# At most four loads open at once on GpSimd's queue, in a linear-attention and token-mixing kernel

## The chip, the cores and the metric

The kernel runs on one core of one Trainium2 chip. The core has a matrix engine (TensorE, PE in the profile), a vector engine (VectorE, DVE), an activation engine (ScalarE, ACT), a general engine (GpSimd, POOL) and a synchronisation engine that issues transfers (SyncE, SP). Each works through its own list of instructions in order; semaphores tie the lists together. Sixteen DMA engines move data between the chip's memory (HBM) and the on-chip buffer (SBUF). TensorE writes to a second on-chip memory of 8 banks (PSUM).

The metric is the time of one execution on the device in microseconds (us); lower is better.

## What is computed

The inputs are q, k and v of shape (4, 8, 768, 64): 4 batches, 8 heads, 768 positions, 64 channels, in float32. The first half is linear attention with a decay `lam` per head, the second mixes the tokens of the result with each other. Cut to what matters:

```python
# attention, in blocks of 64 positions; lam is one number per head
intra = einsum('bhic,bhjc->bhij', qb, kb) * Dmask      # Dmask = lam ** (i - j), lower triangle
intra = einsum('bhij,bhjd->bhid', intra, vb)
inter = einsum('bhid,bhde->bhie', qb * lam ** (pos + 1), kv_state)
out[:, :, block] = intra + inter
kv_state = lam ** 64 * kv_state + einsum('bhsd,bhse->bhde', kb * lam ** (63 - pos), vb)

# token mixing; x is the attention's output as (batch, position, 512)
wq, wk = x @ w_q, x @ w_k                               # 512 -> 64
mixed = einsum('bst,btd->bsd', wq @ wk.T / 8, x)
return relu(mixed) @ w_out
```

## The kernel before, in words

The work is cut into 16 units, n = 0 to 15. A unit is one batch and one pair of heads (4 batches of 4 pairs); both heads lie side by side in 128 partitions or 128 columns. Units 0 to 3 are batch 0, and so on. When the four units of a batch are done, that batch's token mixing can run. The program handles blocks of 128 positions, six to a unit (NCH = 6), and takes the decay into q and v: q at position t is multiplied by lam to the power t, v by lam to the power -t, so that scores need only a triangular mask.

For each unit n there are three loads, `load_q`, `load_k` and `load_v` (lines 111 to 121), each into a buffer of its own (the pool `stage` has 16 of each, so no load waits for a buffer). They are issued by GpSimd, read float32 and write bfloat16, 192 KB on the chip each: q.n into `fq`, k.n into `fk`, v.n into `fv`. GpSimd also loads the three weight matrices (`load_wq`, `load_wk`, `load_wo`).

What sets the order is the text ORDER (lines 29 to 67), written out by hand: its words are read from left to right, each calls one function, and each function appends its instructions to the lists of the engines it uses. In a word, the number behind the dot is the unit, the number behind @ the PSUM bank, the letter behind the colon the engine (a: ScalarE, v: VectorE, p: GpSimd). Since engines run in parallel, only the order of the words that use one engine counts for that engine. For GpSimd that is: the loads q.0, k.0, v.0, q.1, k.1, v.1 (lines 144 to 153, ahead of ORDER), then the first three lines of ORDER. These hold all other loads and, between them, the words `sv.n:p`.

The steps that follow a unit's loads:

- Aq.n and Ak.n (`turn_q`, line 251; `turn_k`, line 260): TensorE transposes q.n and k.n, twelve matrix instructions each. These are the first uses of those loads.
- eq.n and ek.n (lines 266 and 234): VectorE or ScalarE take the transposes out of PSUM; eq.n multiplies by q's decay.
- sv.n (`scale_v`, line 239): v.n times its decay, in place in `fv`, on VectorE or GpSimd. In ORDER, GpSimd does n = 4, 5, 7, 9, 10, 11, 12, 13 and 14; VectorE does the rest. sv.4 stands behind v.7 in the list of GpSimd, sv.5 behind v.8, sv.7 behind v.10, sv.9 behind v.12, sv.10 behind v.13, sv.11 behind v.14, and sv.12, sv.13 and sv.14 behind v.15.
- S0.n and S1.n (line 277): the scores; M0, M1, Mc and Mm (lines 291, 306, 310) mask them.
- P.n (`states`, line 319): TensorE multiplies k.n by the scaled v.n into the running states. It needs sv.n.
- G.n takes the states out; I.n (line 347) and V.n (line 359) form the unit's output in PSUM; ex.n takes it to `xnat`; F.n (line 382) transposes it for the mixing.
- Q, K, Y, m and O with their evictions are the token mixing of a batch; O (line 508) ends in stores of `out` from SyncE.
- Z.n (line 528): n matmuls on a blank tile, early in the kernel, whose results aren't used.
- hold.14: a transfer of 64 elements out of `fk` of unit 14, issued by SyncE. Stores come behind it in SyncE's list.

The transfers of GpSimd's queue tell of their landing through eight semaphores, used in turn.

Of the kernel before, what the change touches and what calls it, by code (L numbers as in the profile page):

```python
# [9 lines left out]
BF16 = mybir.dt.bfloat16  # L10
# [16 lines left out]


ORDER = """
q.2 k.2 v.2 q.3 k.3 v.3 wq.0 wk.0 q.4 k.4 v.4 wo.0 q.5 k.5 v.5 q.6 k.6 v.6 q.7 k.7 v.7 sv.4:p q.8  # L30
k.8 v.8 sv.5:p q.9 k.9 v.9 q.10 k.10 v.10 sv.7:p q.11 k.11 v.11 q.12 k.12 v.12 sv.9:p q.13 k.13
v.13 sv.10:p q.14 k.14 v.14 sv.11:p q.15 k.15 v.15 sv.12:p sv.13:p sv.14:p hold.14 Aq.0@0 dq.2
eq.0@0 dq.3 Z.5@7 Ak.0@0 dq.1 ek.0@0:v Z.3@7 S1.0@0 sv.0:v S0.0@2 Mc.0@2 M1.0@0 Z.3@7 P.0@4 Aq.1@5
G.0@4:a Mm.0:v Z.1@7 I.0@0 eq.1@5 Ak.1@4 V.0@0 ek.1@4:v ex.0@0:a S0.1@4 sv.1:v S1.1@2 Mc.1@4 Z.1@7
F.0@0 M1.1@2 P.1@1 ef.0@0:a Aq.2@4 Mm.1:v G.1@1:a eq.2@4 Z.1@7 Ak.2@0 I.1@2 ek.2@0:v V.1@2 S1.2@0
# [35 lines left out]
def kernel(  # L71
# [11 lines left out]
    nc = tc.nc  # L83
    mm = nc.tensor.matmul

    consts = ctx.enter_context(tc.tile_pool(name="consts", bufs=1))
# [18 lines left out]
    def rows(n, src):  # L105
        b, kk = divmod(n, NP)
        return src[b, 2 * kk : 2 * kk + 2].rearrange("h (c p) d -> p h c d", p=128)

    fq, fk, fv, vn = {}, {}, {}, {}
# [9 lines left out]
    def load_v(n):  # L119
        fv[n] = stage.tile([128, 2, NCH, D], BF16, tag="fv", name="fv")  # L120
        nc.gpsimd.dma_start(out=fv[n], in_=rows(n, v))  # L121

    wqk = consts.tile([128, 4, 3 * DHY], BF16, name="wqk")
    wo = consts.tile([128, 4, HD], BF16, name="wo")
# [14 lines left out]
    def load_wo(_):  # L139
# [8 lines left out]
        row, pattern=[[0, 1]], base=1, channel_multiplier=1, allow_small_or_imprecise_dtypes=True  # L148
    )
    load_v(0)  # L150
    load_q(1)
    load_k(1)
    load_v(1)
    lam_all = consts.tile([128, H], F32, name="lam_all")
    nc.sync.dma_start(out=lam_all, in_=lam.partition_broadcast(128))
# [7 lines left out]
    one = consts.tile([128, 1], F32, name="one")  # L163
# [4 lines left out]
        out=ET[:, 0:CH], data0=step, data1=step, initial=0.0, op0=ALU.add, op1=ALU.bypass  # L168
    )
    for at, n in ((CH, CH), (2 * CH, 2 * CH), (4 * CH, 2 * CH)):  # L170
        nc.vector.tensor_tensor(
            out=ET[:, at : at + n], in0=ET[:, 0:n],
# [5 lines left out]
        out=ident.rearrange("e (p r) -> e p r", r=2), in0=natural,  # L178
# [4 lines left out]
        out=mask1, in0=ET[:, 0:CH], in1=row.to_broadcast([128, CH]), op=ALU.is_ge  # L183
# [4 lines left out]
    for r in range(2):  # L188
        nc.vector.tensor_tensor(
            out=token[R[r], :], in0=token[R[r], :],  # L190
# [5 lines left out]
        out=order.rearrange("e (p r) -> e p r", r=2), in0=natural,  # L196
# [5 lines left out]
        out=E6, in0=ET[:, ::CH], in1=row.to_broadcast([128, NCH]), op=ALU.add  # L202
# [69 lines left out]
    def scores(a):  # L272
        def one(n, o):
            for cc in range(3):
                c = slice((3 * a + cc) * CH, (3 * a + cc + 1) * CH)
                for hl in range(2):
                    mm(  # L277
                        PS[:, o + hl, cc * CH : (cc + 1) * CH],
                        kT[n][R[hl], c],
                        qT[n][R[hl], c],  # L280
                        start=True,
                        stop=True,
                        skip_group_check=True,
                    )

        return one
# [239 lines left out]
    def zeros(count, o):  # L526
# [4 lines left out]
    make_dq(0)  # L531
    make_dv(0)
    pieces = dict(
        q=load_q, k=load_k, v=load_v, wq=load_wq, wk=load_wk, cw=copy_wq, wo=load_wo, hold=hold, dq=make_dq, dv=make_dv,
        sv=scale_v, Aq=turn_q, Ak=turn_k, eq=turned_q, ek=turned_k, S0=scores(0), S1=scores(1),
        M0=masked(0), M1=masked(1), Mc=drawn, Mm=masked_late, P=states, G=summed, I=inter, V=values, ex=attended, F=flip,
        ef=flipped, eg=flipped_half, Q=mix_q, eQ=mixed_q, K=mix_k, eK=mixed_k, Kh=mix_k_half, ek2=mixed_k_half, Y=mix_y, YA=mixed_y, YB=crossed_y(0), YC=crossed_y(1), Qp=mix_q_part, m=mix_m,
# [38 lines left out]
```

## Time and profile before

| | |
|---|---|
| three timed runs, median | 99.39 us (99.37 to 99.69) |
| the profiled execution | 100.16 us |
| its span, first to last instruction | 98.4 us |
| granted TensorE clock, mean over the span | 0.99 |
| GpSimd: 16 issues of q, mean of one, and median to landing | 0.88 us, 7.5 us |
| GpSimd: 16 issues of k, the same | 1.05 us, 8.0 us |
| GpSimd: 16 issues of v, the same | 1.04 us, 8.0 us |
| GpSimd: 9 scalings of v | 1.51 us each |
| VectorE: 7 scalings of v | 1.00 us each |

Times inside the execution count from the span's start. "To landing" is the time from the start of the instruction that issues a transfer until its semaphore says that all of it has arrived. The page divides the span into 40 equal slices and gives each engine's busy share of a slice as a digit, 9 for 90% or more. "The chain" is followed back from the last instruction: at each step to what released it, or to the instruction before it on its engine. A row of a timeline gives start, duration, engine, line, operation, output and input, how many instructions are merged in it and, in brackets, the idle time ahead of it and what ended that.

### The profile page before, as it was taken

What the parts mean: (1) busy time and instruction counts of PE and PEld (TensorE: products, weight loads), DVE (VectorE), ACT (ScalarE), POOL (GpSimd) and SP (SyncE); (2) the same over time, 40 slices, a digit from 0 to 9 for tenths busy, and PEclk for the clock granted to TensorE, in tenths of its full rate; (3) what the DMA queues carried; (4) which work ended last, traced back from release to release, by engine and by line L of the source; (5) the groups of instructions that cost most, each with busy time, mean ns of one, the idle gap of its engine ahead of it and who ended that gap; (6) DMA issues with size and microseconds to landing.
All of it is one profiled execution on the core that took longest, in us unless ns stands there. A gap on an engine that the chain in (4) does not pass through costs nothing.

```text
span 98.4 us, 3425 instructions
## 1 busy us (share of the span) xinstructions
PE 88.8 (90%) x1469; PEld 56.3 (57%) x1469; DVE 72.0 (73%) x140; ACT 61.5 (63%) x101; POOL 61.5 (62%) x65
## 2 busy tenths in 40 slices
PE   5999898699989999999898899999999999999930
PEld 1345674567565667667566587777696754534400
DVE  5738892993889998998798499699999845544200
ACT  5576486158539358378557396776589992493440
POOL 5999996899579999999999999970000000000000
PEclk9999999999999999999999999999999999999996
DMA  0999999999999999999999999999950202545782
GB/s 1 95 143 163 165 156 167 159 167 190 182 164 162 169 161 164 166 162 163 168 162 164 166 164 161 174 223 402 372 188 6 107 7 107 213 154 217 286 308 101
DMA packets 67438, 16.60 MB, mean 169 GB/s; under 512 B 63840, under 2 KB 64352, under 8 KB 67424
## 3 DMA queue, kind: packets, MB, share of 16 engines
q0 software_dynamic: 63792, 10.10, 139.0%
q1 hardware_dynamic: 3632, 6.30, 17.0%
q8 instruction: 11, 0.18, 0.7%
q14 instruction: 3, 0.02, 0.1%
HBM read 20.19 MB, written 6.29 MB: 269 GB/s over the span
## 4 chain that ended last, share of the span: by engine, by line
PE 69%; DMA 8%; POOL 8%; DVE 5%; ACT 3%; issue 3%; POOLq 0%; ACTq 0%
PE ps L508 22%; DMA fv<-in_v_dram 8%; PE ps L359 6%; PE ps L277 6%; PE ps L382 5%; PE ps L319 5%; PE ps L260 5%; PE ps L404 4%; PE ps L251 4%; PE ps L455 3%; POOL fk L117 3%; PE ps L347 3%; POOL fq L113 3%; PE ps L479 2%; POOL fv L121 2%
## 5 line engine op out<-in xcount | busy, mean ns | idle before, releaser
L291 DVE TENSOR_TENSOR pr<-ps,mask 128x768 bf16<-128x768 f32 x28 | 25.9, 950 | 0.8 <-PE ps L277 0.7
L508 PE MATMUL ps<-wo,rmT 128*128 128x512 bf16 x96 | 23.6, 380 | 0.0
L117 POOL DMA_DIRECT2D fk<-in_k_dram x16 | 16.8, 1048 | 1.4 <-DMA wo<-in_moe_w_out_dram 1.3
L121 POOL DMA_DIRECT2D fv<-in_v_dram x16 | 16.7, 1044 | 1.4 <-DMA fv<-in_v_dram 1.0
L234 ACT COPY osb<-ps 128x512 f32<-128x512 f32 x19 | 11.2, 588 | 10.0 <-PE ps L508 8.9
L113 POOL DMA_DIRECT2D fq<-in_q_dram x16 | 14.1, 883 | 1.1 <-POOLq L560 0.8
L234 ACT CAST xnat<-ps 128x768 bf16<-128x768 f32 x13 | 10.4, 799 | 6.6 <-PE ps L359 6.2
L239 POOL TENSOR_TENSOR fv<-fv,DvI 128x768 bf16<-128x768 bf16 x9 | 13.5, 1512 | 0.0
L508 PEld LDWEIGHTS <-rmT 128*128 128x128 bf16 x96 | 8.3, 98 | 8.6 <-issue 0.7
L490 ACT ACTIVATE rmT<-ps 128x768 bf16<-128x768 f32 (+1 forms) x16 | 10.6, 722 | 0.2
L528 PE MATMUL ps<-blank 128*128 128x512 bf16 x29 | 9.5, 445 | 1.2 <-DVE blank L158 1.2
L266 DVE TENSOR_TENSOR qT<-ps,dq 128x768 bf16<-128x768 bf16 x16 | 8.8, 553 | 2.1 <-PE ps L251 2.0
L277 PE MATMUL ps<-qT,kT 64*128 64x128 bf16 x192 | 9.0, 218 | 0.4 <-DVE kT L234 0.3
L234 ACT COPY kT<-ps 128x768 bf16<-128x768 bf16 x9 | 7.2, 799 | 2.9 <-PE ps L260 2.4
L319 PE MATMUL ps<-fv,fk 128*64 128x128 bf16 (+4 forms) x160 | 7.8, 229 | 1.4 <-DVE fv L239 1.4
L359 PE MATMUL ps<-fv,pr 128*128 128x64 bf16 x192 | 8.5, 194 | 0.5 <-issue 0.5
L251 PE MATMUL ps<-ident,fq 128*64 128x128 bf16 x192 | 8.3, 221 | 0.3 <-DVE E L201 0.3
L260 PE MATMUL ps<-ident,fk 128*64 128x128 bf16 x192 | 8.3, 221 | 0.3
L239 DVE TENSOR_TENSOR fv<-fv,DvI 128x768 bf16<-128x768 bf16 x7 | 7.0, 1004 | 1.9 <-DMA fv<-in_v_dram 1.7
L319 PEld LDWEIGHTS <-fk 128*64 128x64 bf16 x160 | 5.9, 110 | 4.1 <-DVE fv L239 2.3
L277 PEld LDWEIGHTS <-kT 64*128 64x128 bf16 x192 | 5.6, 94 | 4.1 <-DVE kT L234 1.5
L359 PEld LDWEIGHTS <-pr 128*128 128x128 bf16 x192 | 6.8, 98 | 1.9 <-issue 0.8
(68 smaller groups left out, 131.2 us busy)
## 6 DMA issues: line engine op xcount, KB each, us to landing
out_dram<-osb SPq DMA_DIRECT2D x24, 256.0 KB, 2.1
fq<-in_q_dram POOLq DMA_DIRECT2D x16, 192.0 KB, 7.5
fk<-in_k_dram POOLq DMA_DIRECT2D x16, 192.0 KB, 8.0
fv<-in_v_dram POOLq DMA_DIRECT2D x16, 192.0 KB, 8.0
wo<-in_moe_w_out_dram POOLq DMA_DIRECT2D x1, 512.0 KB, 8.7
wqk<-in_moe_w_q_dram POOLq DMA_DIRECT2D x1, 64.0 KB, 7.6
wqk<-in_moe_w_k_dram POOLq DMA_DIRECT2D x1, 64.0 KB, 7.3
lam_all<-in_lam_dram SPq DMA_DIRECT2D x1, 4.0 KB, 2.5
```

The costliest lines, as they stand in the source:

```text
L113: nc.gpsimd.dma_start(out=fq[n], in_=rows_q(n))
L117: nc.gpsimd.dma_start(out=fk[n], in_=rows(n, k))
L121: nc.gpsimd.dma_start(out=fv[n], in_=rows(n, v))
L234: return (nc.scalar.copy if eng == "a" else nc.vector.tensor_copy)(out=to, in_=of)
L239: (nc.gpsimd if eng == "p" else nc.vector).tensor_tensor(out=vn[n], in0=fv[n], in1=DvI[:, 2 * kk : 2 * kk + 2, :].unsqueeze(3).to_broadcas ...
L251: nc.tensor.transpose(to.rearrange("e (t r p) -> e r t p", t=2, r=2)[:, r], fq[n][:, hl, a, r * D : (r + 1) * D], ident,)
L260: nc.tensor.transpose(PSH[R[hl], o, c * CH : (c + 1) * CH], fk[n][:, hl, c, :], ident)
L277: mm(PS[:, o + hl, cc * CH : (cc + 1) * CH], kT[n][R[hl], c], qT[n][R[hl], c], start=True, stop=True, skip_group_check=True,)
L291: nc.vector.tensor_tensor(out=pr[n, a].rearrange("j l (c i) -> j l c i", c=3), in0=PS[:, o : o + 2, 0:HALF].rearrange("j l (c i) -> j l c ...
L319: mm(to[R[hl], c:end, :], fk[n][:, hl, c, :], vn[n][:, hl, c, :].unsqueeze(1).to_broadcast([128, end - c, D]), start=(c == 0), stop=(c == ...
L359: mm(PS[:, o + hl, c * D : (c + 1) * D], pr[n, c // 3][:, hl, (c % 3) * CH : (c % 3 + 1) * CH], vn[n][:, hl, c, :], start=False, stop=(c = ...
L508: mm(PS[:, o, :], rmT[b][:, kt].rearrange("f n i -> f (n i)")[:, t * CH : (t + 1) * CH], wo[:, kt, :], start=(kt == 0), stop=(kt == 3),)
```

## The change

GpSimd copies one element of a load's buffer into a scratch tile, `landed`, before it issues another load. Since the copy reads the buffer, it can't run before that load has landed; the issue stands behind it in GpSimd's list. The copy ahead of a load reads the load four back among q, k and v: v.n-2 ahead of q.n, q.n-1 ahead of k.n, k.n-1 ahead of v.n. The first copy stands ahead of q.3. The weights' loads are issued without a copy of their own. All other words keep their order; `sv.n:p` stays directly behind the load that it followed.

```diff
 ORDER = """
-q.2 k.2 v.2 q.3 k.3 v.3 wq.0 wk.0 q.4 k.4 v.4 wo.0 q.5 k.5 v.5 q.6 k.6 v.6 q.7 k.7 v.7 sv.4:p q.8
-k.8 v.8 sv.5:p q.9 k.9 v.9 q.10 k.10 v.10 sv.7:p q.11 k.11 v.11 q.12 k.12 v.12 sv.9:p q.13 k.13
-v.13 sv.10:p q.14 k.14 v.14 sv.11:p q.15 k.15 v.15 sv.12:p sv.13:p sv.14:p hold.14 Aq.0@0 dq.2
+q.2 k.2 v.2 av.1 q.3 aq.2 k.3 ak.2 v.3 wq.0 wk.0 av.2 q.4 aq.3 k.4 ak.3 v.4 wo.0 av.3 q.5 aq.4 k.5 ak.4 v.5 av.4 q.6 aq.5 k.6 ak.5 v.6 av.5 q.7 aq.6 k.7 ak.6 v.7 sv.4:p av.6 q.8
+aq.7 k.8 ak.7 v.8 sv.5:p av.7 q.9 aq.8 k.9 ak.8 v.9 av.8 q.10 aq.9 k.10 ak.9 v.10 sv.7:p av.9 q.11 aq.10 k.11 ak.10 v.11 av.10 q.12 aq.11 k.12 ak.11 v.12 sv.9:p av.11 q.13 aq.12 k.13
+ak.12 v.13 sv.10:p av.12 q.14 aq.13 k.14 ak.13 v.14 sv.11:p av.13 q.15 aq.14 k.15 ak.14 v.15 sv.12:p sv.13:p sv.14:p hold.14 Aq.0@0 dq.2
...
+    landed = consts.tile([1, 1], BF16, name="landed")
+
+    def after(tiles):
+        def one(n):
+            nc.gpsimd.tensor_copy(out=landed, in_=tiles[n][0:1, 0, 0, 0:1])
+
+        return one
...
-        q=load_q, k=load_k, v=load_v, wq=load_wq, wk=load_wk, cw=copy_wq, wo=load_wo, hold=hold, dq=make_dq, dv=make_dv,
+        q=load_q, k=load_k, v=load_v, aq=after(fq), ak=after(fk), av=after(fv), wq=load_wq, wk=load_wk, cw=copy_wq, wo=load_wo, hold=hold, dq=make_dq, dv=make_dv,
```

That is 39 copies. On the other engines the list of instructions stays what it was.

## The prediction

> **What bounds the kernel now.** I read the page from the top, then the chain of waits in order of time, then GpSimd's own timeline, then the time to landing of single loads.
>
> ```profile
> span 98.4 us, 3425 instructions
> PE 88.8 (90%) x1469; PEld 56.3 (57%) x1469; DVE 72.0 (73%) x140; ACT 61.5 (63%) x101; POOL 61.5 (62%) x65
> ...
> POOL 5999996899579999999999999970000000000000
> ...
> DMA  0999999999999999999999999999950202545782
> ...
> PE 69%; DMA 8%; POOL 8%; DVE 5%; ACT 3%; issue 3%; POOLq 0%; ACTq 0%
> ```
>
> TensorE holds 90% of the span and 69% of the chain. GpSimd and the DMA engines are full too, but only for the first 65 to 72 us. So there are two stages: an early one in which loads decide, and a later one in which TensorE decides. The chain in order of time shows where they meet:
>
> ```profile
> 9.09 8.00 DMA fv<-in_v_dram
> 17.09 0.02 issue
> 17.11 0.97 DVE fv L239
> ...
> 31.89 0.57 PE ps L319 x10
> ...
> 43.23 0.38 PE ps L319 x10
> ```
>
> Until 17.09 us the chain is loads; afterwards nearly every piece is TensorE's. From 31.9 us to the last matmul at 94.4 us the windows give TensorE 60.8 us busy of 62.5 (11.10 of 11.10, 22.38 of 24.0, 27.35 of 27.4). It has no spare time there, and it works in program order, so a matmul that waits there moves the end. L319 is the state product P.n; its moving operand is the scaled v.n. For n = 4, 5, 7 and 9 to 14 GpSimd scales v.n (L239), between its own load issues:
>
> ```profile
> 22.36 0.84 POOL L113 DMA_DIRECT2D fq<-in_q_dram  x1
> 23.17 1.04 POOL L117 DMA_DIRECT2D fk<-in_k_dram  x1
> ...
> 27.36 1.02 POOL L117 DMA_DIRECT2D fk<-in_k_dram  x1 [1.32 <-DMA wo<-in_moe_w_out_dram]
> 28.73 1.01 POOL L121 DMA_DIRECT2D fv<-in_v_dram  x1 [0.35 <-issue]
> 29.75 1.48 POOL L239 TENSOR_TENSOR fv<-fv,DvI 128x768 bf16<-128x768 bf16 x1
> 31.17 0.89 POOL L113 DMA_DIRECT2D fq<-in_q_dram  x1
> ...
> 41.23 1.54 POOL L239 TENSOR_TENSOR fv<-fv,DvI 128x768 bf16<-128x768 bf16 x1
> ...
> 61.34 4.36 POOL L239 TENSOR_TENSOR fv<-fv,DvI 128x768 bf16<-128x768 bf16 x3
> ```
>
> Counting loads from the start, these are q.6, k.6, k.7, v.7, then sv.4, q.8; sv.7; and sv.12 to sv.14. The reader is to see that from 28.7 us on nothing separates GpSimd's rows: it has no spare time either. Each scaling ends just before its product starts:
>
> ```profile
> 31.86 0.60 PE L319 MATMUL ps<-fv,fk 128*64 128x320 bf16 x10
> ...
> 43.16 0.45 PE L319 MATMUL ps<-fv,fk 128*64 128x128 bf16 x10
> ...
> 67.17 0.42 PE L319 MATMUL ps<-fv,fk 128*64 128x128 bf16 x10
> ```
>
> These are P.4, P.7 and P.13. sv.4 ends at 29.75 + 1.48 = 31.23, which leaves 0.6 us to P.4; sv.7 ends at 42.77, 0.4 us before P.7; sv.13, the second of the last three, ends at 61.34 + 2 x 1.45 = 64.25, 2.9 us before P.13. The fourth view is the landing of one load, k.6, issued at 23.17:
>
> ```profile
> fk<-in_k_dram POOLq DMA_DIRECT2D x1, 192.0 KB, 10.1
> ```
>
> It lands at 33.3 us, 10 us after its issue and 4.5 us after v.7 was issued. GpSimd runs about eight loads ahead of the landings. Asked in the same way, the first load takes 3.8 us to land, k.7 9.4, v.15 6.6; landings follow each other at about 1.2 us all the way.
>
> [...]landings keep the order of issue, 1.2 us apart, whether 4 or 10 us after it. [...]after the last matmul, which ends at 94.4, the granted clock is 0.72 in the stretch from 96 to 97 and 0.50 from 97 to 98. [...]
>
> **The change part by part.** No transfer, matmul or vector operation is removed or exchanged. GpSimd gets 39 copies of one element, each waiting for the landing of the load four back among q, k and v; each sits ahead of the next issue.
>
> Early loads (up to k.6). q.2, k.2 and v.2 are issued as before, so v.2 still lands at 17.09. Later issues slip by 1 to 5 us, but do they starve the queue? An issue needs about 1.7 us to its first packet (q.0: issued 1.25, traffic starts at 3.0). With 0.3 us to wake (v.2 lands at 17.09, the issue that waits for it starts at 17.38) and a copy, a new load is at the engines some 2.1 us after the landing of the load four back, while three loads of 1.2 us, less the 0.8 us by which a landing trails its last packet (q.0: 3.0 + 1.2 = 4.2, landed 5.05), are 2.8 us of work. The queue stays fed by 0.7 us; even with the two weight loads and `wo` between, I find no landing up to k.6 that moves. Early cost nothing; bounds: 0 to 0.5 us.
>
> sv.4. Behind the copy that waits for k.6 stand v.7, sv.4 and everything after them. v.7 can start at 33.3 + 0.3 + copy. The copy: lower bound 0.05 us (the four memsets of 0.10 us start 0.03 apart), upper bound 0.30 (the iota of 0.18, which with its setup delays v.0's issue by 0.18, plus a second wait ahead of it); I take 0.12, a little above the memset's 0.10, because it must read. It can't be below nothing, as an instruction is added. So v.7 starts at 33.7 instead of 28.73: GpSimd is 5.0 us late. sv.4 ends at 36.2, and P.4 waits from 31.86: 4.3 us. Queued behind P.4 on TensorE is all that is left of the kernel.
>
> From there GpSimd is bound by itself. Between v.7 and v.15 there are 24 issues, six scalings and now 24 copies; before, that stretch had no gap, and landings come early enough (an issue lands after about 4 us, four issues and copies take longer). So its lateness grows by one copy per load. At sv.7 nine copies: 5.0 + 1.1 = 6.1 late, end 48.9, P.7 at 43.16 needs it: 5.7 us late. At sv.9, sv.10 and sv.11, which ended at 49.9, 54.2 and 58.5 for products at 52.1, 57.0 and 62.6, the same sum gives 4.6, 4.4 and 3.4. At sv.13 24 copies: 5.0 + 2.9 = 7.9, end 72.15 against 67.17: 5.0. These aren't added: each is a shift of TensorE against before, and the largest holds. Between P.7 and P.13 TensorE has gaps of 0.54 and 0.69 us that a late TensorE might close; then 4.5 would be left of the 5.7 and P.13's 5.0 takes over. After P.13 there's 27.35 busy in 27.4, so nothing comes back. The sum is +5.0 to +5.7; I take +5.4.
>
> Clock. A gap of 4.3 us at P.4 is likely to halve the clock. [...]
>
> Loads for q and k past v.7 land later too, by 0 to 5 us, but the slack to their transposes (1 us at k.7, 6 at q.15) grows by TensorE's own shift; they hide. v.15, scaled by VectorE at 70.7, lands near 72 against a need at 76. Output stores are issued from 62.9 us; they move with TensorE.
>
> The profiled execution took 100.16 us, 98.4 of span and 1.76 around it. It becomes 105.6. The three timed runs have a median of 99.39, 0.77 lower, so the same sum gives 104.8.
>
> **Rivals.** First, copies are dear (0.30): lateness at sv.13 is 5.2 + 7.2 = 12.4, less 2.9 of slack, +9.5, 108.9 us. For it: GpSimd has no gap to take them in. Against: the memsets cost little. Second, the stall is partly taken back: VectorE and ScalarE catch up while TensorE waits, and copies cost 0.05; +2.5, 101.9. Against: TensorE is 11.10 busy of 11.10 right after P.4. Third, faster: fewer open loads make each packet quicker[...]. The place is the first 17 us, where TensorE idles 1.36 us for v.2 and some 0.8 for k.0 and q.0; the gain is at most those, about -1.5 us, 97.9. It decides only if k.6 lands before 29 us, 4.3 earlier, so that sv.4 isn't late: loads then have to come a fifth faster. Against: the windows give 169 GB/s from 3.5 to 4.4 us, with three loads open, and 164 from 33 to 36 us, with some seven. Fourth, the cap doesn't bind, because the waits are already met: 99.4. Against: landing of k.6 at 33.3 lies behind v.7's issue at 28.73.
>
> **How the numbers follow.** Forecast case 0.72, dear copies 0.12, taken back 0.08, faster 0.05, no effect 0.03. The time is 104.8. The forecast's own bounds are: copy 0.05 gives P.7 +5.0, of which 1.2 may be closed, +3.8 or 103.2; copy 0.30 gives 108.9. The range 102.8 to 109.0 takes both in, with a little below; outside are the other three cases. A measurement of this kernel tells a change from none at about 0.3%, 0.3 us. Faster 0.05, same 0.03, slower 0.92.
>
> **What would show it.** In the changed profile: v.7's issue near 33.7 after a copy that waits for k.6's landing near 33.3; TensorE idle for about 4 us before P.4, released by GpSimd's L239 scaling; a second wait before P.7 and one before P.13; GpSimd's last row near 73.5 instead of 65.7; time to landing near 4 to 5 us instead of 8; the same landing of v.2. Wrong would be: k.6 landing well before 31 us (shorter queues do speed transfers), landings up to k.6 later than before (the queue runs dry), copies over 0.3 us, or a TensorE gap before P.4 and an end that hardly moves.

## The result, and the profile after

The changed kernel takes 113.75 us (median of 4 runs, 112.89 to 113.88), the one before 99.54 beside it: a ratio of 1.139, 95% interval 1.130 to 1.148. The change costs 14.2 us; the forecast was 5.4, with a range that ended at 109.0. The profiled execution took 113.72 us, 111.9 of span. Below, medians take in all runs of a kernel, but ratios and their intervals leave out the few executions that were over 1.5% slower than its fastest.

First the page of the changed kernel, with the lines that answer to those shown of before:

```profile
span 111.9 us, 3493 instructions
PE 89.8 (80%) x1455; PEld 57.8 (52%) x1469; DVE 72.1 (64%) x140; ACT 61.8 (55%) x101; POOL 68.8 (61%) x104
...
POOL 6996599994087999979994999999700000000000
PEclk9999999999997555999999999999999999999996
DMA  0999999999999999999999999999998020344883
...
POOL 31%; DMA 27%; PE 23%; issue 11%; ACT 2%; POOLq 1%; DVE 1%; ACTq 0%
```

TensorE's busy time is the same within 1 us (88.8 before), so no work was added to it; it waits. On the chain it went from 69% to 23%, and GpSimd and the DMA engines together from 16% to 58%. The line PEclk shows three slices at half the clock, which fell at about 35 us. The DMA digits look as full as before, but they show the time that packets took, with several under way at once (a share of 1.72 and 2.02 in the windows of experiment 2), not what was delivered. The packets are the same 16.6 MB, in a span that is 13.5 us longer.

GpSimd's timeline around v.7 (start, duration, engine, line, operation, and idle time with what ended it):

```profile
25.77 0.82 POOL L113 DMA_DIRECT2D fq<-in_q_dram  x1 [0.21 <-issue]
30.68 0.18 POOL L128 COPY landed<-fq 1x1 bf16<-1x1 bf16 x1 [4.09 <-DMA fq<-in_q_dram]
31.14 1.01 POOL L117 DMA_DIRECT2D fk<-in_k_dram  x1 [0.28 <-issue]
...
35.84 0.18 POOL L128 COPY landed<-fk 1x1 bf16<-1x1 bf16 x1
36.44 1.01 POOL L121 DMA_DIRECT2D fv<-in_v_dram  x1 [0.42 <-issue]
37.47 1.49 POOL L248 TENSOR_TENSOR fv<-fv,DvI 128x768 bf16<-128x768 bf16 x1
...
76.16 4.33 POOL L248 TENSOR_TENSOR fv<-fv,DvI 128x768 bf16<-128x768 bf16 x3
```

These are q.6, the copy that waits 4.1 us for q.5, k.6, then the copy that waits for k.6, v.7, sv.4, and sv.12 to sv.14. sv.4 starts at 37.47 instead of 29.75, 7.7 us late; the last three start 14.8 us late. The list of waits names who pays:

```profile
PE ps L328 <- POOL fv L248: 8.8, 4, 5.4
...
POOL landed L128 <- DMA fq<-in_q_dram: 4.1, 1, 4.1
...
DVE fv L248 <- POOL landed L128: 2.8, 3, 2.0
```

(Columns: total in us, times, longest.) TensorE waits four times for a scaling by GpSimd: 5.4 us at P.4, 1.9 at P.9, 0.5 at P.10 and 1.1 at P.13. The third line is a wait that the prediction didn't have: VectorE scales v in place, so it may not start before GpSimd's copy has read the buffer. Last, three loads of the changed kernel, asked for singly, `wo`, k.6 and v.15:

```profile
wo<-in_moe_w_out_dram POOLq DMA_DIRECT2D x1, 512.0 KB, 8.4
...
fk<-in_k_dram POOLq DMA_DIRECT2D x1, 192.0 KB, 4.5
...
fv<-in_v_dram POOLq DMA_DIRECT2D x1, 192.0 KB, 9.2
```

Issued at 21.05, 31.14 and 75.13 us, they land at 29.5, 35.6 and 84.3. Before, `wo` landed at 27.1, k.6 at 33.2 and v.15 at 66.9.

One number is used below for every kernel, the pace of the loads: the landing of k.14 less that of k.6, divided by the 24 loads between them. Before, (62.2 - 33.2) / 24 = 1.21 us; in the changed kernel (74.4 - 35.6) / 24 = 1.61 us.

### The profile page after: what moved, and what is told of

Same layout as the page of the kernel before. It is cut to its first block, busy times and chain, and to the rows that moved or that the text cites. A ratio compares the mean times of both kernels' runs of the same rounds, so it can differ in the third digit from the quotient of the medians.

```text
span 111.9 us, 3493 instructions
## 1 busy us (share of the span) xinstructions
PE 89.8 (80%) x1455; PEld 57.8 (52%) x1469; DVE 72.1 (64%) x140; ACT 61.8 (55%) x101; POOL 68.8 (61%) x104
## 4 chain that ended last, share of the span: by engine, by line
POOL 31%; DMA 27%; PE 23%; issue 11%; ACT 2%; POOLq 1%; DVE 1%; ACTq 0%
DMA fq<-in_q_dram 17%; PE ps L517 12%; POOL fq L113 7%; POOL fk L117 7%; POOL fv L121 6%; POOL landed L128 6%; DMA fv<-in_v_dram 5%; POOL fv L248 5%; DMA fk<-in_k_dram 5%; PE ps L413 2%; PE ps L488 2%; PE ps L391 1%; POOLq L580 1%; PE ps L464 1%; PE ps L368 1%
## 5 line engine op out<-in xcount | busy, mean ns | idle before, releaser
L328 PE MATMUL ps<-fv,fk 128*64 128x128 bf16 (+4 forms) x160 | 8.4, 236 | 12.5 <-POOL fv L248 8.8
L117 POOL DMA_DIRECT2D fk<-in_k_dram x16 | 16.3, 1016 | 1.0 <-issue 1.0
L328 PEld LDWEIGHTS <-fk 128*64 128x64 bf16 x160 | 6.8, 112 | 15.4 <-issue 11.7
L537 PE MATMUL ps<-blank 128*128 128x512 bf16 x25 | 8.2, 450 | 1.5 <-DVE blank L167 1.2
L391 PE MATMUL ps<-order,xnat 128*128 128x128 bf16 x96 | 7.8, 220 | 0.2 <-ACT xnat L243 0.2
L260 PEld LDWEIGHTS <-fq 128*64 128x64 bf16 x192 | 6.3, 113 | 3.0 <-DMA fq<-in_q_dram 1.9
```

The lines of the kernel that those rows point to most:

```text
L117: nc.gpsimd.dma_start(out=fk[n], in_=rows(n, k))
L260: nc.tensor.transpose(to.rearrange("e (t r p) -> e r t p", t=2, r=2)[:, r], fq[n][:, hl, a, r * D : (r + 1) * D], ident,)
L328: mm(to[R[hl], c:end, :], fk[n][:, hl, c, :], vn[n][:, hl, c, :].unsqueeze(1).to_broadcast([128, end - c, D]), start=(c == 0), stop=(c == ...
L391: nc.tensor.transpose(PSH[:, o, c * CH : (c + 1) * CH], xnat[b][:, c, kk * CH : (kk + 1) * CH], order,)
```

## The experiments

Theory A, as in the prediction: the loss is the place of the scalings, behind issues that wait, in a list that is full. Rivals: B, the copies are dear; C, the halved clock; D, with few open the loads themselves come too slowly. Some expectations speak of theory R, which is D with a mechanism and is put together in experiment 5, and of theory L: that GpSimd's copies and wake-ups set the pace of the loads. The edits are to the changed kernel unless it says otherwise.

**1. Copies that wait for nothing**

```diff
-            nc.gpsimd.tensor_copy(out=landed, in_=tiles[n][0:1, 0, 0, 0:1])
+            nc.gpsimd.tensor_copy(out=landed, in_=fk[0][0:1, 0, 0, 0:1])
```

> All 39 copies stay where they are but read k.0, which landed at 6.8 us, so none of them waits; this is the price of the copies alone. Theory A (the loss comes from loads that wait for landings, and from the scalings that stand behind them in GpSimd's list): GpSimd is late by 0.12 us per copy, about 1.1 us at sv.7 and 2.9 us at sv.13, of which the slack takes nearly all; 99.5 to 101 us. Rival B (the copies themselves are dear, or GpSimd's reads get in the way of its issues): most of the loss stays, over 107 us.

Measured: 101.64 us, ratio 1.019 (1.011 to 1.027). GpSimd's timeline of this run:

```profile
43.59 0.88 POOL L113 DMA_DIRECT2D fq<-in_q_dram  x1
44.47 0.18 POOL L128 COPY landed<-fk 1x1 bf16<-1x1 bf16 x1
44.59 1.01 POOL L117 DMA_DIRECT2D fk<-in_k_dram  x1
45.59 0.18 POOL L128 COPY landed<-fk 1x1 bf16<-1x1 bf16 x1
45.71 1.01 POOL L121 DMA_DIRECT2D fv<-in_v_dram  x1
```

From k's issue to v's it is 1.12 us where it was 1.00: a copy holds the list for 0.12 us although it is recorded with 0.18, because the next issue starts before it ends. From v.7 to v.15 GpSimd now takes 34.5 us (28.46 to 62.96) instead of 31.6; the loads keep their pace of 1.21. The price is as forecast, the end a little above the expectation. Rival B falls: 2 us of the 14.2.

**2. The clock**

```diff
- ... P.4@0 ...
+ ... Z.20@0 P.4@0 ...
```

> The changed kernel with twenty more blank matmuls (4.3 us at full clock) ahead of P.4, inside the 5.4 us for which TensorE waits there, so that the clock isn't halved afterwards. Theory A: TensorE is held by GpSimd's scalings again at P.9 and P.13, so it loses the time gained: clock back to about 0.99, end within 0.6 us of the changed kernel (113.7). Rival C (the halved clock from 34.9 to 45.1 us is a part of the loss that lasts): 3 us of work at half rate come back, 110 to 111 us.

Measured: 114.61 us, 1.153 (1.146 to 1.161). The mean granted clock of the profiled execution is 1.000 (0.945 in the changed kernel), and nothing is gained. Rival C falls for the end. What the halved clock does is visible in the windows of the changed kernel (columns: span, busy us and count of TensorE, of its weight loads, VectorE, ScalarE and GpSimd, granted clock, DMA share, GB/s):

```profile
34.90:39.00 4.10, 0.00 (x0) 0.00 (x0) 0.00 (x0) 0.00 (x0) 3.66 (x5) 0.50 2.02 147
39.00:45.10 6.10, 5.71 (x60) 3.70 (x62) 3.52 (x5) 2.05 (x3) 6.08 (x10) 0.50 1.72 123
```

TensorE runs at a granted clock of 0.50 for 6 us after P.4. With the clock kept, it comes to P.7 earlier and waits there instead, which it doesn't in the changed kernel:

```profile
53.65 0.42 PE L328 MATMUL ps<-fv,fk 128*64 128x128 bf16 x9 [3.01 <-POOL fv L248]
```

**3. Stores held one load longer**

```diff
- ... sv.14:p hold.14 ...
+ ... sv.14:p hold.15 ...
```

> The changed kernel with SyncE's stores held until k.15 has landed instead of k.14; v.15 is issued by then. In the changed kernel the stores start at 75 us and k.15 and v.15 need 7.1 and 9.2 us to land. If the stores that overtake these loads are what makes P.15 wait 1.4 us: v.15 lands about 5 us after its issue, the last gap goes, 112.3 us. If not, or if the stores' later start costs as much: 113.7 or more.

Measured: 112.58 us, 1.130 (1.122 to 1.138), 1.2 us under the changed kernel; the two intervals overlap, so the traces decide. v.15, issued at 75.94, takes

```profile
fv<-in_v_dram POOLq DMA_DIRECT2D x1, 192.0 KB, 4.7
```

instead of 9.2 us, and lands at 80.7 instead of 84.3. The stores did hold up the last load; P.15's wait of 1.4 us is gone too. Before the change, all loads had been issued when k.14 landed and the stores were let go; with the cap, k.15 and v.15 were issued at about the same time as the stores (74.00 and 75.13, the stores from 75.02 us). What this is worth at the end, about 1 us, the intervals don't settle.

**4. VectorE's scaled v in tiles of its own**

```diff
-        vn[n] = fv[n]
+        vn[n] = fv[n] if eng == "p" else stage.tile([128, 2, NCH, D], BF16, tag=f"vn{n}", bufs=1, name="vn")
```

> The changed kernel, but VectorE's scalings of v (n = 0, 1, 2, 3, 6, 8, 15) write to a tile of their own instead of in place, so that they needn't wait until GpSimd's copy has read the buffer. TensorE should be at P.3 about 1.2 us earlier (23.0 to 21.8). Theory A: the end is set by GpSimd's list from P.4 on, so the time stays within 0.5 us of 113.7. Rival: the early 1.2 us last to the end, 112.5.

Measured: 113.99 us, 1.139 (1.129 to 1.149). P.3 comes at 21.6 instead of 23.0 us, as expected, and the end doesn't move. The wait of VectorE for the copies is real, and hidden by what comes later.

**5. The scalings left out**

```diff
         vn[n] = fv[n]
+        if eng == "p":
+            return
```

> The changed kernel with GpSimd's nine scalings of v left out (v.4, v.5, v.7 and v.9 to v.14 stay without their decay factor); copies, waits and loads stay. Theory A (TensorE waits because the scalings stand behind the held-back issues and fill GpSimd's list): the waits at P.4, P.9 and P.13 go, GpSimd keeps up with the landings; what is left is q.5, about 2.3 us late behind the weight load, and the last v loads: 101.5 to 104 us. Rival D (with four open the loads themselves arrive too slowly): at least half of the 14.2 us stays, over 106.5.

Measured: 111.18 us (109.71 to 116.02), 1.107 (1.093 to 1.121), far above the 104 us that theory A allowed. Without any scaling on GpSimd, only about 3 us of the 14.2 come back at the end (a loss of 10.7% instead of 13.9), so theory A fell as the whole cause. The page of this run, with its chain by engine and its time to landing:

```profile
DMA 47%; PE 21%; POOL 17%; issue 10%; DVE 1%; ACT 1%; POOLq 0%; ACTq 0%
...
fq<-in_q_dram POOLq DMA_DIRECT2D x16, 192.0 KB, 5.4
fk<-in_k_dram POOLq DMA_DIRECT2D x16, 192.0 KB, 5.4
fv<-in_v_dram POOLq DMA_DIRECT2D x16, 192.0 KB, 5.4
```

GpSimd is only 50% busy, and the loads come every 1.52 us ((71.8 - 35.3) / 24), so TensorE waits for q and k themselves. From one landing to the start of the issue that waited for it the trace has 0.6 us (the landing of q.9 at 47.87, its copy at 47.99, the issue of k.10 at 48.44), and no issue from q.8 on starts later than 0.92 us after its landing. A turn is thus 5.4 + 0.6 = 6.0 us, and four loads share it: 1.5 us each. That is theory R, rival D with a mechanism: four open loads don't cover the round trip. The sum alone proves nothing: wherever each issue follows a landing at once, the turn is four times the pace, whatever sets the pace. Experiments 9 to 11 change the number open.

The time at the end mixes two things. These are P.13, VectorE's scaling of v.15, and P.15:

```profile
73.37 0.42 PE L330 MATMUL ps<-fv,fk 128*64 128x128 bf16 x10
...
80.64 0.96 DVE L250 TENSOR_TENSOR fv<-fv,DvI 128x768 bf16<-128x768 bf16 x1 [3.69 <-DMA fv<-in_v_dram]
...
82.25 0.69 PE L330 MATMUL ps<-fv,fk 128*64 128x128 bf16 x10 [3.48 <-DVE gs L348]
```

P.13 started at 67.17 us before the change and at 79.11 in the changed kernel, 11.9 late; here it is 6.2 late, so half of that is gone. But v.15, issued at 72.52 beside stores that start at 72.40, takes 8.1 us to land, and TensorE waits 3.5 us for P.15 instead of 1.4. It looks like the collision of experiment 3 again, but no run takes it out of this kernel.

**6 and 7. The cap in one half only.** Without the 15 copies ahead of the loads up to v.7 (late), or without the 24 from q.8 on (early):

```diff
- q.2 k.2 v.2 av.1 q.3 aq.2 k.3 ... ak.6 v.7 sv.4:p av.6 q.8 aq.7 k.8 ...
+ q.2 k.2 v.2 q.3 k.3 ... v.7 sv.4:p av.6 q.8 aq.7 k.8 ...           (late)
+ q.2 k.2 v.2 av.1 q.3 aq.2 k.3 ... ak.6 v.7 sv.4:p q.8 k.8 ...      (early)
```

> No copy ahead of any load up to v.7, all 24 from q.8 on. Up to sv.4 GpSimd is as before, so P.4 doesn't wait and the clock stays full. From there the first copy waits for v.6 (34.4 us), q.8 is issued at about 35 instead of 31.2 us. Theory A, by GpSimd's list: 3.7 us late at q.8, and the lateness grows by the copies and by the landings waited for, as in the changed kernel (from 7.7 at sv.4 to 14.8 at sv.13, +7.1), to about 10 at sv.13, less 2.9 of slack, and about 1 for v.15: 107 to 109 us. Rival (the early part sets the loss): under 104.

> The 15 copies up to v.7, none after. GpSimd is 7.7 us late at sv.4 as in the changed kernel, then runs without copies and waits: the lateness stays at 7.7 at most and falls where the eight landing semaphores had made it wait. Theory A: TensorE 7.2 us late at P.4, the halved clock adds up to 3 us until about 45 us, nothing later adds: 107 to 110 us. If the parts of the loss simply add up, this run and the one with the late cap alone lose together more than 14.2 us, as each hides some of the other.

Measured: late 109.56 us (107.65 to 110.26), 1.088 (1.073 to 1.103); early 107.59, 1.080 (1.072 to 1.089). Each half alone costs more than half of the whole, 8.8 and 8.0%, against 13.9 for both: they hide each other. In the late run `wo` lands at 27.0 and sv.4 starts at 29.6, as before the change, and the loads then come every 1.57 us. So there are two separate delays, one before v.7 and one after.

**8. Six open instead of four**

```diff
- ... av.3 q.5 aq.4 k.5 ak.4 v.5 ...
+ ... aq.3 q.5 ak.3 k.5 av.3 v.5 ...
```

> All 39 copies, each reading the load six back instead of four. Theory A: v.7 waits for v.5 (30.7) instead of k.6, is issued at about 31.6, sv.4 ends at 34, P.4 is 2.2 us late; few waits for landings after; with the copies 101.6 (measured without waits) plus 2 to 3: 103 to 105 us. If the time depended on the transfers' own rate with a shorter queue, six open would lose about half of what four lose, 106 or more.

Measured: 104.41 us, 1.049 (1.041 to 1.057). From v.7 to v.15 GpSimd takes 35.3 us (31.97 to 67.23), close to the 34.5 of the copies that don't wait: with six open its list alone sets the pace. With four it takes 38.7 us (36.44 to 75.13), so waits come on top of the list.

**9, 10 and 11. The round trip by itself.** Six and three open, and no cap at all, each without the nine scalings (the edit of 5), so that GpSimd has time:

```diff
- ... av.6 q.8 aq.7 k.8 ak.7 v.8 ...          (four)
+ ... aq.6 q.8 ak.6 k.8 av.6 v.8 ...          (six)
+ ... aq.7 q.8 ak.7 k.8 av.7 v.8 ...          (three)
```

> Six open instead of four, GpSimd's nine scalings of v left out (v.4, v.5, v.7 and v.9 to v.14 without their decay factor). Theory R (round trip): with n loads open, n landings take one turn of issue to landing (about 5.4 us in the run with four and no scalings) plus landing to next issue (0.6 us); so from k.6 to k.14 1.52 us per load with four, and with six the engines' own 1.2 us bounds: 1.2 to 1.25 us per load, 100.5 to 102.5 us. Theory L (GpSimd's list, its copies and wake-ups set the rate): the same number of copies and waits, 1.45 to 1.5 us per load, 108 us or more.

> Three open, the nine scalings left out. Theory R: an unloaded load of k or v takes 4.7 us to land, plus 0.6 to the next issue is 5.3; a third of it, 1.75 to 1.8 us per load from k.6 to k.14 (four: 1.52), and the time goes up by 24 to 30 loads times 0.25 us, 116 to 120 us. Theory L: the rate stays about 1.5 us, within 2 us of the run with four (111.2).

> The kernel before with the same nine scalings left out, as the base for the other runs without them. TensorE bounds it from 32 us on, so 98.5 to 99.5 us; loads from k.6 to k.14 at 1.2 us each or a little less.

| without the scalings | time, us | ratio to before, interval | to landing, us | pace of the loads, us | P.13 starts, us | wait at P.15, us |
|---|---|---|---|---|---|---|
| three open | 121.68 | 1.225 (1.217 to 1.234) | 4.5 | 1.70 | 80.4 | 3.4 |
| four open | 111.18 | 1.107 (1.093 to 1.121) | 5.4 | 1.52 | 73.4 | 3.5 |
| six open | 99.33 | 0.997 (0.995 to 1.000) | 6.5 | 1.21 | 66.2 | none |
| no cap | 100.29 | 1.008 (1.004 to 1.012) | 9.2 | 1.20 | 66.1 | none |

("To landing" is the median for k.) With three, (4.5 + 0.6) / 3 = 1.70; with four, (5.4 + 0.6) / 4 = 1.50; with six the pace is that of no cap. The same copies stand in the first three rows, so neither they nor the wake-ups make the pace (theory L): the number open does, and P.13, which stands ahead of the collision with the stores, moves with it. A load with little else open takes 4.6 to 4.7 us to land (k.0 and v.0 before the change), which would give 1.8 for three and 1.3 for four. Three fits; why four open loads take 5.4 us each, at a pace of 1.52 us where the kernel without a cap has 1.20, stays open. The chain by engine, three open and then six:

```profile
DMA 55%; PE 20%; POOL 13%; issue 8%; DVE 1%; ACT 0%; POOLq 0%; ACTq 0%
```

```profile
PE 65%; POOL 18%; DVE 5%; issue 5%; ACT 3%; POOLq 0%; ACTq 0%
```

With six, TensorE carries the chain again, as before the change. The three-open run came out slower than the expectation by some 2 us, at a pace a little better than expected: the expectation had no wait at P.15. The six-open run came out 1.2 us faster than expected, the one without a cap 0.8 slower.

**12. The scalings where nothing waits ahead of them**

```diff
- ... v.5 av.4 q.6 ... ak.6 v.7 sv.4:p av.6 q.8 ...
+ ... v.5 av.4 sv.4:p q.6 ... ak.6 v.7 av.6 q.8 ...
```

> The changed kernel, computing all, with each of GpSimd's scalings moved directly behind the copy that has seen its load land (sv.4 behind av.4, and so on), so that none stands behind a load that waits. The waits for scalings at P.4, P.9 and P.13 should go. Theory R: loads still come at 1.5 to 1.6 us each, TensorE waits for them instead: 110.5 to 113.5 us. Theory A as first put (the place of the scalings is the loss): under 107 us.

(sv.14 stays behind v.15, which is the last load.) Measured: 116.46 us, 1.168 (1.162 to 1.173), 2.7 us worse than the changed kernel and outside both expectations. The waits of this run, TensorE's own (PE and its weight loads) and VectorE's:

```profile
PEld L267 <- DMA fk<-in_k_dram: 7.0, 7, 2.4
DVE fv L246 <- DMA fv<-in_v_dram: 6.5, 2, 6.2
...
PE ps L267 <- DMA fk<-in_k_dram: 5.5, 5, 2.3
...
PEld L258 <- DMA fq<-in_q_dram: 5.0, 4, 2.8
```

No scaling by GpSimd holds TensorE any more; the loads do, at a pace of 1.65 us ((75.0 - 35.4) / 24). A scaling ahead of an issue now stands inside the turn from landing to issue, which would explain why this is more than the 1.52 without scalings; it wasn't taken apart. These are P.13, the first use of k.15, and P.15:

```profile
75.61 0.42 PE L326 MATMUL ps<-fv,fk 128*64 128x128 bf16 x10
...
82.74 0.53 PE L267 MATMUL ps<-ident,fk 128*64 128x128 bf16 x12 [2.32 <-DMA fk<-in_k_dram]
...
87.00 0.69 PE L326 MATMUL ps<-fv,fk 128*64 128x128 bf16 x10 [3.48 <-DVE gs L344]
```

P.13 comes 3.5 us earlier than in the changed kernel (79.11), and is still 8.4 later than before the change. That the end is worse comes behind it: k.15 and v.15, issued at 75.66 and 76.79 beside stores from 75.69 us, take 7.0 and 8.6 us to land, and TensorE waits 2.3 us for the one and 3.5 for the other. So the place of the scalings is worth 3.5 of the 11.9 us at P.13: theory A is a part of the loss, not the whole. No run combines this edit with later stores. No experiment pointed to a version that computes all and beats the kernel before.

## Why the prediction was right or wrong

Right: slower, and that earlier landings would not pay for it. v.2, which I had estimated to land as before, lands at 16.9 against 17.1 us, and of the later loads only q.3 and k.3 came sooner, by 0.5 and 0.3 us. A copy costs 0.12 us of GpSimd's list, as taken, with two exceptions below. P.4 waits for sv.4, which stands behind v.7 and the copy for k.6, and TensorE is held again before P.9, P.10 and P.13. The wait forecast at P.7 is hidden by the halved clock, which costs nothing at the end (experiment 2).

Wrong, the step that failed: "landings come early enough (an issue lands after about 4 us, four issues and copies take longer)", and with it "From there GpSimd is bound by itself". A time of 3.8 us to land is that of q.0 alone. k.0 and v.0, with one and two loads open ahead of them, needed 4.6 and 4.7 us in the same trace. In the changed kernel the 24 loads from k.6 to v.13 take 4.9 us on average, and at least 0.6 us to the next issue come on top: 5.5 us. Four loads' share of GpSimd's list, with copies, is 4 x 34.5 / 24 = 5.8 us. The forecast thus had 1.8 us to spare in each turn where there were 0.3, and single loads take 3.5 to 6.0 us. So the two limits take turns, and the pace is slower than either: four times the measured 1.61 us is 6.4, 4.9 to land and 1.5 to the next issue. Of the 24 issues from q.8 on only four start within 0.6 us of the landing that they wait for (v.10, v.12, k.14 and v.14); at the others the landing is past and the list is behind. The longest such wait is the copy ahead of v.12:

```profile
60.17 0.18 POOL L128 COPY landed<-fk 1x1 bf16<-1x1 bf16 x1 [1.44 <-DMA fk<-in_k_dram]
```

GpSimd's lateness so grows by 38.7 - 31.6 = 7.1 us from v.7 to v.15 instead of 2.9: 2.9 for the copies, as forecast, about 2.8 at these four landings, and 1.2 in two copies that have nothing to wait for. Their loads had landed 2.0 and 1.4 us before, but VectorE was scaling v at the time:

```profile
44.27 0.95 DVE L248 TENSOR_TENSOR fv<-fv,DvI 128x768 bf16<-128x768 bf16 x1
44.60 0.67 POOL L128 COPY landed<-fq 1x1 bf16<-1x1 bf16 x1
...
52.59 0.99 POOL L128 COPY landed<-fv 1x1 bf16<-1x1 bf16 x1
52.59 0.95 DVE L248 TENSOR_TENSOR fv<-fv,DvI 128x768 bf16<-128x768 bf16 x1
```

Each copy ends within 0.05 us of the end of VectorE's scaling. Experiments 5, 9 and 10 show what landings alone do where GpSimd has time. The rival that a faster or slower transfer rate would decide was set up for a gain only; a stream slowed by its own round trip was not among the cases.

Wrong, earlier in the list: "I find no landing up to k.6 that moves". The sum there compared 2.1 us from a landing to the next load's first packets with 2.8 us of work in the queue; it took `wo` as just another load. `wo` lands 8.2 to 9.1 us after its issue in all fourteen traces, whatever stands ahead of it, so its landing moves with its issue, and the cap delays that by 2.7 us (21.05 for 18.38). It lands 2.4 us later than before, and q.5, on which the copy ahead of k.6 waits, comes behind it at 30.6 instead of 28.2. From 24 to 26 us the windows give 129 GB/s at a DMA share of 1.05, where the kernel before has 195 at 1.39. That landings up to k.6 come later was the prediction's own sign that the queue runs dry. So sv.4 is 7.7 us late, not 5.0: 2.3 for k.6's landing, the rest from wake-up to issue (0.8 us instead of 0.42). With six open `wo` lands at 27.6, without the early cap at 27.0: it goes with the cap. Why `wo` takes that long was not isolated.

Wrong, a collision: "Output stores are issued from 62.9 us; they move with TensorE", and v.15 "lands near 72". The stores are let go by k.14's landing, and with the cap the last loads haven't all been issued by then. v.15 took 9.2 us, P.15 waited 1.4. Experiment 3 took that wait away; its 1.2 us at the end lie within overlapping intervals.

Not in the prediction: VectorE's in-place scaling waits for the copy's read. Shown (P.3 by 1.4 us), and without effect on the end (experiment 4).

By place, TensorE's shift against before was 7.2 us at P.4 (39.01 for 31.86), 11.9 at P.13 (79.1 for 67.17) and 13.5 at the end of the span. The forecast had 4.3, 5.0 and 5.4. At P.13 the 11.9 are GpSimd's 14.8 less the 2.9 of slack that the forecast also had; P.15's 1.4 make nearly all of the rest.

## What to carry to other kernels

A cap on open transfers was a rate here, where it bound: loads open, divided by the time from issue to landing plus the time from landing to the next issue. Without the scalings, three open give a load every (4.5 + 0.6) / 3 = 1.70 us and four every (5.4 + 0.6) / 4 = 1.50; the traces have 1.70 and 1.52. Work that out with the slowest kind of load (here `wo`, with 8.4 us to land in the changed kernel against 4.9 for the loads from k.6 to v.13), and with what else the issuing engine does inside the turn, before asking which instruction stands behind which. Where that turn and the engine's own list came out nearly equal (5.5 and 5.8 us), neither hid the other: four loads took 6.4. Where two steps both seem to hold an engine back, take one out, and read the effect ahead of whatever else the change sets off: here removing the visible wait gave 5.7 of 11.9 us at P.13, because the stream behind it was nearly as slow, and only about 3 of 14.2 at the end, where v.15, issued beside the stores, took 8.1 us to land.

## What the runs showed that I had not expected

- The granted clock, once halved, stayed so from 34.87 to 45.11 us, 10.2 us, and in the last 6.1 of them TensorE had nearly full work (39.0 to 45.1 us, 5.71 busy). In experiment 1 the stretch at half clock lasts 3.4 us (31.93 to 35.34), in experiment 3 6.8 (38.31 to 45.14); the mean granted clocks of the three profiled executions are 0.945, 0.973 and 0.964. What sets the length of such a stretch was not shown.
- In the changed kernel, the four copies of one element on GpSimd that start well inside a scaling of v by VectorE (at 18.50, 22.74, 44.60 and 52.59 us) last 0.27, 0.27, 0.67 and 0.99 us, where most others are recorded with 0.18, and each ends within 0.05 us of the scaling's end. In experiment 8 such a copy took 0.96 us (46.97 to 47.93, the scaling 46.94 to 47.89).
- Without the nine scalings the uncapped kernel is 0.8% slower than the kernel before (100.29 us), though it does less, and the one with six open is not (99.33). Their intervals are apart (1.004 to 1.012, 0.995 to 1.000). TensorE carries the chain in both; what makes the difference wasn't tried.
